# First routing phase with one operation between digits, and a changed order of side work in a fused retention, expert and gated-unit kernel

## The chip, the cores and the metric

The kernel runs on one core of a Trainium2 chip. The metric is the device time of one execution in microseconds (us), taken as the median of the runs shown. TensorE is PE in the profile (its weight loads PEld), VectorE is DVE, ScalarE is ACT, GpSimd is POOL, SyncE is SP. Each engine works through its own instructions in the order in which the program emits them; what one engine needs of another it waits for by semaphores.

## The reference, cut to what matters

Retention over 4 batches, 8 heads, 768 steps and 64 channels gives 3072 tokens of 512 values. The tokens are then dealt to 8 experts, and what the experts give goes through a gated unit with 1536 hidden columns:

```
logits = x @ w_gate                      # 3072 x 8
for idx in argsort(-logits.flatten()):   # best pair of token and expert first
    tok, e = idx // E, idx % E
    if assigned[tok] >= 0 or counts[e] >= cap: continue      # cap = 384
    assigned[tok] = e; counts[e] += 1
for e in range(E):
    out[assigned == e] = relu(x[assigned == e] @ w1[e]) @ w2[e]
gate = sigmoid(out @ w_gate2);  val = out @ w_val
return (gate * val) @ w_out
```

## The kernel before, in words

**Attention** (to about 154 us) works through 24 chunks of 128 tokens. In its spare time 23 of the 36 blocks of the gated unit's weights, which lie as 64-bit numbers in memory, are converted to 32 bits by `conv_steps`: step one is ACT L153 and DVE L154, step two DVE L156, step three ACT L158 and POOL L159, step four DVE L161. The other 13 are converted later (`late`, below).

**Routing** deals one expert at a time: the expert that fills up first, and its 384 tokens. `members(x)` does it. For the first expert (x = 0) nothing else can run beside it: five digits of a threshold are found one after the other (`widths`), each by three compares on DVE (`compare`, one for each third of the chunks in `parts`), 24 small matmuls (`count`, L284), a maximum (L587), a matmul with ones (L593) and two operations that make the next digit's column `edb` (L596, L598). `keep_busy` puts matmuls without use between them. Then a prefix sum (L624), another set of compares, a count and the row numbers `idx` (L651), with which three indirect DMAs on POOL's queue fetch the tokens (`gather`, L506).

For the later experts `members(x + 1)` runs while expert x computes, one step at each call of `hook()`; a step yields the number of hooks until the next. Its search has eight digits of 4 bits (`search4`): a compare (L291), three matmuls (L299), three DVE operations that end in `ex` (L301 to L304), a matmul (L318), then five more up to the next digit's compare (L321 to L291, L266). The member search that runs beside the first expert (x == 1) yields 2 hooks between `ex` and L318, the later ones 1.

**Expert and gated unit.** For each expert: 8 `h_step` and 8 `y_step` (w1 with ReLU, w2), then 12 rounds of `g_step` (two products, wg and wv) and `o_step` (wo). Every product is taken in three parts, so each weight block is split into a high part (ACT L664) and a remainder (DVE L665), up to 5 pieces ahead (`ahead`). Every step is some 12 matmuls, or 9 in `o_step`. A hook follows each step: 15 hooks in the `h_step` and `y_step` part (0 to 14), 15 and 16 in the first `g_step`, then three to a round: 17 + 3g, 18 + 3g and 19 + 3g. `h_step` and `y_step` emit what follows their matmuls (the ReLU and the remainder on DVE, the next pieces) and then the hook. `late` hangs the 13 remaining conversions on the hooks of the first expert, from hook 7 every 2.5 hooks. `turn_x` transposes the next expert's tokens (L673) from round 7 on, in the first expert from round 8.

The steps above for x == 1 place the fetch of its tokens at hook 40 and its first transpose right before hook 43; for later experts at hooks 33 and 40 (job[1] = 0; prep at hook 1; digit k's compare at hook 3 + 4k or 3 + 3k; the row numbers and the fetch 9 hooks after the last digit's compare).

**The end.** The last expert's three blocks of output are copied from PSUM (ACT, DVE, ACT) and scattered by three indirect DMAs on POOL's queue (L797).

Of the kernel before, what the change touches and what calls it, by code (L numbers as in the profile page):

```python
# [15 lines left out]
OP = mybir.AluOpType  # L16
# [4 lines left out]
def retention_moe_glu_kernel(  # L21
# [167 lines left out]
    bits = consts.tile([128, 2, NCH], I32, name="bits")  # L189
    far_up = consts.tile([128, NCH], F32, name="far_up")  # L190
    ones16 = consts.tile([128, 128], F16, name="ones16")
    same = consts.tile([128, 8], F32, name="same")
    spread = consts.tile([128, 16], F32, name="spread")

    def late_consts():
        im = dict(allow_small_or_imprecise_dtypes=True)
        POOL.iota(iota1, pattern=[[1, 128]], base=1, channel_multiplier=0, **im)
        POOL.iota(cp[:, :, 0], pattern=[[1, NCH]], base=0, channel_multiplier=0, **im)
        POOL.iota(cp[:, :, 1], pattern=[[0, NCH]], base=0, channel_multiplier=1, **im)
        POOL.iota(w8, pattern=[[-1, E]], base=E, channel_multiplier=0, **im)  # L200
        DVE.tensor_scalar(before, jp, 0.0, None, op0=OP.is_gt)
        DVE.tensor_scalar(after, jp, 0.0, None, op0=OP.is_lt)
        DVE.memset(ones, 1.0)
        DVE.memset(ones_r, 1.0)
        DVE.memset(ones16, 1.0)
        DVE.memset(bits[:, 0, :], -2147483648)
        DVE.memset(bits[:, 1, :], 15)
        DVE.memset(far_up, 512.0)
        DVE.tensor_reduce(same, ident.rearrange("p (t c) -> p c t", c=8), AX, OP.max)
        DVE.tensor_reduce(spread, ident.rearrange("p (t c) -> p t c", c=8), AX, OP.max)  # L210
        DVE.memset(free, 1.0)
        for t in cmp_tiles:
            POOL.memset(t, 0.0)
        DVE.tensor_copy(iox, iota1[:, :, None].to_broadcast([128, 128, NCH]))
        DVE.tensor_copy(arow, w8)
# [7 lines left out]
    NL = len(widths)  # L223
    parts = ((0, 8), (8, 16), (16, 24))
    first_part = ((0, 10), (10, 20), (20, 24))
# [81 lines left out]

    def search4(x):

        for n in range(8):  # L310
# [4 lines left out]
            ex = count4(cm)  # L315
            yield 2 if x == 1 else 1
            pd = psm.tile([128, 128], F32, name="pr")
# [119 lines left out]

    EARLY = 23
    LATE = [7 + 5 * n // 2 for n in range(NP - EARLY)]
    RAWS = 3  # L440
    conv_at = {4 + n * 41 // EARLY: n for n in range(EARLY)}
# [61 lines left out]

    idxs, xT, W, XG = {}, {}, {}, {}
    def gather(dst, src, col):
        POOL.indirect_dma_start(out=dst, out_offset=None, in_=src,  # L506
                                in_offset=bass.IndirectOffsetOnAxis(ap=col, axis=0))
# [32 lines left out]
    def fetch_rest():  # L540

        rest = W[0][0][:, :, 512:]
        ACT.activation(rest[:, 0, :1], ident[:, :1], AF.Copy)
        src = w1[bass.ds(which[0], 1)].rearrange("o (a p) f -> p (o a) f", p=128)
        SP.dma_start(rest, src[:, :, 512:])
        for f in range(2, W2R):
            fetch_w2(0, f)
        for n in range(RAWS):
            conv_load(EARLY + n, main, RAWS)

    which = {}

    def members(x, begun=None):
# [10 lines left out]
        if x < E - 1:  # L564
# [7 lines left out]
            for n in range(NL if x == 0 else 0):  # L572
# [6 lines left out]
                if n + 1 < NL:  # L579
                    digit(n + 1)  # L580
                yield 3 if T > 64 else 2
                pr = psm.tile([128, 128], F32, name="pr")
# [9 lines left out]
                if n + 1 < NL:  # L592
                    PE.matmul(pd[:, 0:1], ones[:T, :], fb[:T], start=True, stop=True)  # L593
                    wait(WA)
                    ed = small("ed")
                    DVE.tensor_scalar(ed, r["edb"], pd[:, 0:1], 512.0, op0=OP.subtract, op1=OP.mult)  # L596
                    r["edb"] = small("edb", dt=BF)
                    DVE.tensor_tensor(r["edb"], ed, r["dig"][:, n + 1, :], OP.add)  # L598
            if x == 0:
                full = pd[:, 0:E]  # L600
                PE.matmul(full, ones, fl, start=True, stop=True)
                wait(WC)
            else:
                yield from search4(x)
                full = r["full"]
# [14 lines left out]
        idxs[x] = idx  # L620
        DVE.tensor_scalar(which[x], mx[:1], -1.0, float(E), op0=OP.mult, op1=OP.add)
        sc = small("sc", (128, 2, NCH), BF)
        scf = sc.rearrange("p a c -> p (a c)")
        DVE.tensor_tensor_scan(scf, ones_r, AE.rearrange("p a c -> p (a c)"), 0.0, OP.mult, OP.add)  # L624
        fetch_weights(x)
        yield 2
# [16 lines left out]
        cms = [compare(i, c0, c1, 128, smb, OP.is_equal) for i, (c0, c1) in enumerate(parts)]  # L643
        yield 3 if x == 1 else 4
        ps = psm.tile([128, 128], F32, name="pr")
# [7 lines left out]
        if x + 1 < E:  # L653
            far = small("far")
            DVE.scalar_tensor_tensor(far, ai, NA - 0.5, free, op0=OP.is_gt, op1=OP.mult)
            DVE.scalar_tensor_tensor(free, ai, -0.5, free, op0=OP.is_lt, op1=OP.mult)
            DVE.tensor_tensor(free, free, far, OP.add)
            r["pen"] = small("pen", (128, E))
            DVE.tensor_scalar(r["pen"], w8, mx, -3.0e38, op0=OP.is_equal, op1=OP.mult)
            DVE.scalar_tensor_tensor(arow, arow, mx, arow, op0=OP.not_equal, op1=OP.mult)  # L660
        yield 1

# [35 lines left out]
    def make(n):  # L698
        while made[0] < min(n, len(order)):
# [11 lines left out]
            t = main.tile([128, 2, DT, 128], F32R, name="piece", bufs=RING)  # L711
            split(src, t[:, 0], t[:, 1], DVE)
            pieces[key] = t
# [18 lines left out]
    def h_step(x, f):  # L732
        w = use(("w1", x, f))
        p = psm.tile([128, CAP], F32, name="mm", bufs=3)
        for dt in range(DT):
            three(p, w, (xT[x][:, 0, dt, :], xT[x][:, 1, dt, :]), dt, dt == 0, dt == DT - 1)
        t = main.tile([128, 2, CAP], F32R, name="hT", bufs=2)
        ACT.activation(t[:, 0], p, AF.Relu)  # L738
# [4 lines left out]
    def y_step(x, f):  # L743
# [3 lines left out]
        for dt in range(DT):  # L747
            three(acc[0][dt], w, (hT[f][:, 0], hT[f][:, 1]), dt, f == 0, f == FB - 1)
        if f == FB - 1:
            t = main.tile([128, 2, DT, CAP], F32R, name="x2T")  # L750
            x2[0] = t
            for dt in range(DT):
                split(acc[0][dt], t[:, 0, dt, :], t[:, 1, dt, :])
        ahead(("w2", x, f))

    def g_step(x, g):
        t = x2[0]
        ps = []
        for kind in ("wg", "wv"):
            w = use((kind, x, g))  # L760
            p = psm.tile([128, CAP], F32, name="mm", bufs=3)
            for dt in range(DT):
                three(p, w, (t[:, 0, dt, :], t[:, 1, dt, :]), dt, dt == 0, dt == DT - 1)
            ps.append(p)
            hook()
            if kind == "wg":
                sg = main.tile([128, CAP], F32, name="sg", bufs=2)
                ACT.activation(sg, p, AF.Sigmoid)
        gv = main.tile([128, CAP], F32, name="gv", bufs=2)
        DVE.tensor_tensor(gv, ps[1], sg, OP.mult)  # L770
        gt = main.tile([128, 2, CAP], F32R, name="gT", bufs=2)
        split(gv, gt[:, 0], gt[:, 1])
        gT[g] = gt
        ahead(("wv", x, g))

    scat = []
    spacer = consts.tile([1, 1], F32, name="spacer")

    def o_step(x, g):
        w = use(("wo", x, g)).rearrange("p z a b -> p z (a b)")  # L780
        if g == 0:
            acc[1] = [psm.tile([128, M], F32, name="acc", bufs=4) for _ in range(NA)]
        for a in range(NA):
            r = slice(a * 128, (a + 1) * 128)
            p = acc[1][a]
            PE.matmul(p, gT[g][:, 0, r], w[:, 0], start=(g == 0), stop=False)  # L786
            PE.matmul(p, gT[g][:, 0, r], w[:, 1], start=False, stop=False)  # L787
            PE.matmul(p, gT[g][:, 1, r], w[:, 0], start=False, stop=(g == GB - 1))  # L788
        if g == GB - 1:
            for a in range(NA):  # L790
                o = main.tile([128, M], F32, name="o", bufs=3)
                if a % 2:
                    DVE.tensor_copy(o, acc[1][a])
                else:
                    ACT.activation(o, acc[1][a], AF.Copy)
                POOL.memset(spacer, 0.0)
                st = POOL.indirect_dma_start(  # L797
                    out=out, out_offset=bass.IndirectOffsetOnAxis(ap=idxs[x][:, a:a + 1], axis=0),
                    in_=o, in_offset=None)
                for s in scat:  # L800
                    tc.declare_no_dep(st.ins, s.ins, reason="rows of other tokens")
                scat.append(st)
        ahead(("wo", x, g))
# [28 lines left out]

    late = {}
    for n, u in enumerate(LATE):
        m = EARLY + n
        if n + RAWS < len(LATE):
# [5 lines left out]
    for x in range(E):  # L842
# [4 lines left out]
        for f in range(FB):  # L847
            if f + 1 < FB:
                h_step(x, f + 1)
                hook()  # L850
            y_step(x, f)
            hook()
        g_step(x, 0)
        turn = None
        for g in range(GB):
            if g + 1 < GB:
                g_step(x, g + 1)
            elif x + 1 < E:
                for _ in turn:
                    pass  # L860
                h_step(x + 1, 0)
            if g == (7 if x else 8) and x + 1 < E:
                assert job[0] is None
                turn = turn_x(x + 1)
            if turn is not None:
                next(turn, None)
            o_step(x, g)
            hook()

# [41 lines left out]
```

## Time and profile before

| | |
|---|---|
| median of 3 runs | 1124.16 us (1123.57 to 1124.96) |
| the profiled execution | 1123.29 us |
| its span from first to last instruction | 1121.5 us |
| mean granted TensorE clock | 0.99 of full speed |
| PE busy, share of the span | 1088.5 us, 97% |
| DVE busy | 736.8 us, 66% |
| ACT busy | 487.6 us, 43% |
| POOL busy | 134.9 us, 12% |

Busy shares are means over stages with different limits. PE's matmuls are pipelined and overlap in the records, so that 97% does not mean that PE is at its peak; matmuls without use count too.

### The profile page before, as it was taken

The numbers are of one execution on the slowest core, as the hardware profiler recorded it, in microseconds if no ns is written. First come the engines' busy times: TensorE is split into PE (matmuls) and PEld (weight loads), VectorE is DVE, ScalarE is ACT, GpSimd is POOL, SyncE is SP. The second block draws the span as 40 slices with busy tenths as digits, with TensorE's granted clock in tenths as the row PEclk, the third lists the DMA queues.
The fourth block names the chain that finished last, engine by engine and source line by source line (L and its number), as shares of the span: only waits on it lengthen the run. The fifth ranks groups of instructions, "written<-read, shape, count | busy, mean of one in ns | idle before, by whom it ended". The sixth has DMA issues, their size and how long they took to land.

```text
span 1121.5 us, 18122 instructions
## 1 busy us (share of the span) xinstructions
PE 1088.5 (97%) x6964; PEld 1005.2 (90%) x6964; DVE 736.8 (66%) x1787; ACT 487.6 (43%) x955; POOL 134.9 (12%) x146
## 2 busy tenths in 40 slices
PE   8999999988799999999999999999999999999997
PEld 6988988977799999989998999999989999999996
DVE  4887876888667756775677666765676545554542
ACT  3666623554343444334434343344343434343442
POOL 4354401121110011001100110011001000100001
PEclk9999989999899999999999999999999999999999
DMA  9999916123320212012100310031103012101000
GB/s 218 282 261 292 247 39 217 57 75 87 120 76 1 101 31 75 1 57 76 66 11 10 122 57 20 1 132 47 30 1 132 17 60 79 54 23 54 1 1 29
DMA packets 109608, 91.42 MB, mean 82 GB/s; under 512 B 54737, under 2 KB 92625, under 8 KB 109521
## 3 DMA queue, kind: packets, MB, share of 16 engines
q1 hardware_dynamic: 105680, 77.67, 23.4%
q0 software_dynamic: 3840, 12.59, 3.4%
q8 instruction: 55, 0.90, 0.3%
q14 instruction: 33, 0.26, 0.1%
HBM read 77.66 MB, written 12.58 MB: 80 GB/s over the span
## 4 chain that ended last, share of the span: by engine, by line
PE 73%; issue 11%; DVE 11%; SPq 2%; ACT 1%; DMA 1%; POOL 1%; POOLq 0%; DVEq 0%; ACTq 0%
PE mm L726 13%; PE mm L728 12%; PE mm L727 12%; PE acc L786 5%; PE acc L788 5%; PE acc L787 5%; DVE piece L665 3%; PE acc L726 2%; PE acc L728 2%; PE acc L727 2%; PE pA L373 2%; PE pY L388 2%; PE pX L407 2%; PE pS L395 2%; PE pY L384 2%
## 5 line engine op out<-in xcount | busy, mean ns | idle before, releaser
L726 PE MATMUL mm<-x2T,piece 128*128 128x384 f32 x768 | 261.7, 341 | 0.4 <-ACT x2T L664 0.4
L728 PE MATMUL mm<-x2T,piece 128*128 128x384 f32 x768 | 258.4, 337 | 0.7 <-DVE x2T L665 0.7
L727 PE MATMUL mm<-x2T,piece 128*128 128x384 f32 x768 | 257.6, 335 | 0.0
L665 DVE TENSOR_TENSOR piece<-wall,piece 128x512 fp32r<-128x512 f32 x288 | 186.2, 689 | 0.0
L664 ACT ACTIVATE gT<-gv 128x384 fp32r<-128x384 f32 x96 | 50.5, 526 | 266.5 <-DVE gv L770 266.5
L664 ACT ACTIVATE piece<-wall 128x512 fp32r<-128x512 f32 x288 | 163.1, 617 | 0.0
L726 PEld LDWEIGHTS mm<-x2T,piece 128*128 128x128 f32 x768 | 144.5, 188 | 3.8 <-ACT x2T L664 0.7
L727 PEld LDWEIGHTS mm<-x2T,piece 128*128 128x128 f32 x768 | 144.4, 188 | 3.1
L728 PEld LDWEIGHTS mm<-x2T,piece 128*128 128x128 f32 x768 | 144.1, 188 | 1.0 <-DVE x2T L665 1.0
L770 DVE TENSOR_TENSOR gv<-mm,sg 128x384 f32<-128x384 f32 x96 | 53.1, 553 | 129.1 <-PE mm L728 127.9
L786 PE MATMUL acc<-piece,gT 128*128 128x512 f32 x288 | 117.5, 408 | 0.0
L788 PE MATMUL acc<-piece,gT 128*128 128x512 f32 x288 | 114.0, 396 | 0.0
L787 PE MATMUL acc<-piece,gT 128*128 128x512 f32 x288 | 113.4, 394 | 0.0
L738 ACT ACTIVATE hT<-mm 128x384 fp32r<-128x384 f32 x64 | 31.5, 492 | 151.7 <-PE mm L728 151.7
L739 DVE SCALAR_TENSOR_TENSOR hT<-mm,hT 128x384 fp32r<-128x384 f32 x64 | 35.7, 557 | 87.1 <-ACT hT L738 87.0
L665 DVE TENSOR_TENSOR gT<-gv,gT 128x384 fp32r<-128x384 f32 x96 | 54.3, 566 | 56.9 <-ACT gT L664 56.9
L726 PE MATMUL mm<-xT,piece 128*128 128x384 f32 x256 | 87.5, 342 | 1.0 <-ACT xT L664 1.0
L726 PE MATMUL acc<-hT,piece 128*128 128x384 f32 x256 | 86.9, 339 | 0.0
L728 PE MATMUL mm<-xT,piece 128*128 128x384 f32 x256 | 86.2, 337 | 0.4 <-DVE xT L665 0.3
L727 PE MATMUL mm<-xT,piece 128*128 128x384 f32 x256 | 85.8, 335 | 0.0
L728 PE MATMUL acc<-hT,piece 128*128 128x384 f32 x256 | 85.8, 335 | 0.0
L727 PE MATMUL acc<-hT,piece 128*128 128x384 f32 x256 | 85.6, 334 | 0.0
(163 smaller groups left out, 1780.2 us busy)
## 6 DMA issues: line engine op xcount, KB each, us to landing
w2s<-in_moe_w_dram SPq DMA_DIRECT2D x64, 256.0 KB, 2.7
w1s<-in_moe_w_dram SPq DMA_DIRECT2D x7, 2048.0 KB, 7.7
q<-in_q_dram SPq DMA_DIRECT2D x12, 512.0 KB, 5.9
k<-in_k_dram SPq DMA_DIRECT2D x24, 256.0 KB, 5.6
v<-in_v_dram SPq DMA_DIRECT2D x24, 256.0 KB, 5.7
raw<-in_moe_w_gate_dram SPq DMA_DIRECT2D x12, 512.0 KB, 5.3
raw<-in_moe_w_val_dram SPq DMA_DIRECT2D x12, 512.0 KB, 5.4
xd<-xs SPq DMA_DIRECT2D x24, 256.0 KB, 4.4
```

The lines of the kernel that those rows point to most:

```text
L373: PE.matmul(ps[s][:, a, :], kT[i][r, a, :], q_of(i)[r, a, :], start=True, stop=True)
L664: ACT.activation(hi, src, AF.Copy)
L665: eng.tensor_tensor(lo, src, hi.bitcast(F32), OP.subtract)
L726: PE.matmul(p, w[:, 0, dt, :], r[0], start=start, stop=False)
L727: PE.matmul(p, w[:, 1, dt, :], r[0], start=False, stop=False)
L728: PE.matmul(p, w[:, 0, dt, :], r[1], start=False, stop=stop)
L738: ACT.activation(t[:, 0], p, AF.Relu)
L739: DVE.scalar_tensor_tensor(t[:, 1], p, 0.0, t[:, 0].bitcast(F32), op0=OP.max, op1=OP.subtract)
L770: DVE.tensor_tensor(gv, ps[1], sg, OP.mult)
L786: PE.matmul(p, gT[g][:, 0, r], w[:, 0], start=(g == 0), stop=False)
L787: PE.matmul(p, gT[g][:, 0, r], w[:, 1], start=False, stop=False)
L788: PE.matmul(p, gT[g][:, 1, r], w[:, 0], start=False, stop=(g == GB - 1))
```

## The change

It has seven parts.

1. First routing phase: the matmul with ones becomes one with 512 (`ones512`), `pre = 512 * edb + next digit` is made while PE counts, and one DVE operation instead of two makes the next `edb`. `parts` goes from 8, 8, 8 chunks to 6, 8, 10. The operation for `which` goes behind the prefix sum.
2. Three of the 13 late conversions move to the first routing phase: their loads are issued where the main pools are opened, and their steps by `fill` in stated places. Two last steps fall on hooks 0 and 1.
3. The other 10 are hung on hooks 7, 10, ... 34.
4. The search beside the first expert yields 1 hook between `ex` and L318, and 4 instead of 3 before the last count, as for the later experts; its `turn_x` starts at round 7.
5. In the first expert the 12 remainders of wo go to POOL.
6. Hooks go inside the steps: in `h_step`, `y_step` and `o_step` ahead of what follows the matmuls; in `g_step` the next pieces go ahead of the hook and of gv and gT.
7. The end: in the last expert the last gv and gT are made in three column blocks, the products of the last two rounds are interleaved (`last_blocks`), and each copy is halved between ACT and DVE.

```diff
-    parts = ((0, 8), (8, 16), (16, 24))
+    parts = ((0, 6), (6, 14), (14, 24))
...
-            yield 2 if x == 1 else 1
+            yield 1
...
-    EARLY = 23
-    LATE = [7 + 5 * n // 2 for n in range(NP - EARLY)]
-    RAWS = 3
+    EARLY, RAWS = 23, 3
+    LATE = [7 + 3 * n for n in range(NP - EARLY - RAWS)]
...
+    for n in range(RAWS):
+        conv_load(EARLY + n, main, RAWS)
+
+    fills = [[], [(0, 1)], [(0, 2)], [(1, 1)], [(0, 1)], [(1, 2), (2, 3)]]
+
+    def fill(x):
+        if x == 0:
+            for n, k in fills.pop(0):
+                conv_step(EARLY + n, k)
...
                 if n + 1 < NL:
                     digit(n + 1)
+                    pre = small("pre")
+                    DVE.scalar_tensor_tensor(pre, r["edb"], 512.0, r["dig"][:, n + 1, :], op0=OP.mult, op1=OP.add)
+                if n:
+                    fill(x)
                 yield 3 if T > 64 else 2
...
-                    PE.matmul(pd[:, 0:1], ones[:T, :], fb[:T], start=True, stop=True)
+                    PE.matmul(pd[:, 0:1], ones512[:T, :], fb[:T], start=True, stop=True)
                     wait(WA)
-                    ed = small("ed")
-                    DVE.tensor_scalar(ed, r["edb"], pd[:, 0:1], 512.0, op0=OP.subtract, op1=OP.mult)
                     r["edb"] = small("edb", dt=BF)
-                    DVE.tensor_tensor(r["edb"], ed, r["dig"][:, n + 1, :], OP.add)
+                    DVE.tensor_scalar(r["edb"], pre, pd[:, 0:1], None, op0=OP.subtract)
...
         cms = [compare(i, c0, c1, 128, smb, OP.is_equal) for i, (c0, c1) in enumerate(parts)]
-        yield 3 if x == 1 else 4
+        fill(x)
+        yield 4
...
+        fill(x)
         yield 1
...
-            split(src, t[:, 0], t[:, 1], DVE)
+            split(src, t[:, 0], t[:, 1], POOL if kind == "wo" and x == 0 else DVE)
...
@@ h_step
+        if f:
+            hook()
         t = main.tile([128, 2, CAP], F32R, name="hT", bufs=2)
...
@@ y_step
+        if f < FB - 1:
+            hook()
         if f == FB - 1:
...
+            hook()
         ahead(("w2", x, f))
...
@@ g_step
+            if kind == "wv":
+                ahead(("wv", x, g))
             hook()
...
+        last = x == E - 1 and g == GB - 1
+        for c in ([slice(a * 128, (a + 1) * 128) for a in range(NA)] if last else [slice(0, CAP)]):
+            DVE.tensor_tensor(gv[:, c], ps[1][:, c], sg[:, c], OP.mult)
+            split(gv[:, c], gt[:, 0, c], gt[:, 1, c])
         gT[g] = gt
-        ahead(("wv", x, g))
...
+    def store(x, a):
+        o = main.tile([128, M], F32, name="o", bufs=3)
+        if x == E - 1:
+            ACT.activation(o[:, :256], acc[1][a][:, :256], AF.Copy)
+            DVE.tensor_copy(o[:, 256:], acc[1][a][:, 256:])
...
+    def last_blocks(x):
+        for g, a in ((GB - 2, 0), (GB - 2, 1), (GB - 1, 0), (GB - 2, 2), (GB - 1, 1), (GB - 1, 2)):
+            o_products(x, g, a)
+            if g == GB - 1:
+                store(x, a)
...
-    late = {}
+    late = {0: [(conv_step, EARLY + 1)], 1: [(conv_step, EARLY + 2)],
+            3: [(conv_load, EARLY + RAWS + 1, main, RAWS), (conv_load, EARLY + RAWS + 2, main, RAWS)]}
...
-            if g == (7 if x else 8) and x + 1 < E:
+            if g == 7 and x + 1 < E:
                 turn = turn_x(x + 1)
```

## Rows read from the trace of the kernel before

**Rows 1.** View by stretches, of before: start:end, length, busy us (instructions) of each engine, clock, DMA

```profile
220.00:240.00 20.00, 18.22 (x102) 16.64 (x103) 18.20 (x45) 10.74 (x20) 4.26 (x3) 1.00 0.20 56
460.00:480.00 20.00, 19.55 (x116) 18.07 (x115) 14.71 (x47) 7.74 (x17) 0.00 (x0) 1.00 0.01 1
296.00:300.20 4.20, 4.20 (x13) 3.52 (x14) 1.29 (x2) 1.11 (x2) 0.41 (x2) 0.56 0.40 120
```

**Rows 2.** Timeline of ACT: start, length, engine, line, operation, [idle before, releaser]

```profile
218.82 1.61 ACT L664 ACTIVATE x2T<-acc 128x384 fp32r<-128x384 f32 x4
...
350.35 2.06 ACT L664 ACTIVATE x2T<-acc 128x384 fp32r<-128x384 f32 x4 [1.21 <-PE acc L728]
...
465.71 2.06 ACT L664 ACTIVATE x2T<-acc 128x384 fp32r<-128x384 f32 x4 [1.21 <-PE acc L728]
```

**Rows 3.** Waits of PE in 184:300: total us, times, longest

```profile
PE mm L673 <- DMA xg<-xd,idx: 6.1, 1, 6.1
PE pr L299 <- DVE cm L291: 4.0, 3, 1.5
PE pr L629 <- DVE sc L624: 1.4, 1, 1.4
PE pr L318 <- DVE ex L304: 1.1, 1, 1.1
```

**Rows 4.** Timeline of DVE in the first expert

```profile
229.23 0.22 DVE L301 TENSOR_TENSOR own<-pr,same 128x64 f32<-128x64 f32 x1
...
230.01 0.69 DVE L161 SCALAR_TENSOR_TENSOR wall<-raw,wall 128x512 f32<-128x512 f32 x1
...
235.37 0.28 DVE L321 TENSOR_REDUCE top<-pr 128x16 f32<-128x128 f32 x1
...
236.75 0.42 DVE L154 TENSOR_SCALAR wall<-raw 128x512 int32<-128x512 int32 x1
...
258.10 1.88 DVE L665 TENSOR_TENSOR piece<-wall,piece 128x512 fp32r<-128x512 f32 x3
```

**Rows 5.** Groups by line, 184:300: count, busy us, mean ns, idle before

```profile
L156 DVE SCALAR_TENSOR_TENSOR wall<-raw,wall 128x512 int32<-128x512 int32 x13 | 9.0, 692 | 0.4
L161 DVE SCALAR_TENSOR_TENSOR wall<-raw,wall 128x512 f32<-128x512 f32 x13 | 8.9, 683 | 0.0
...
L154 DVE TENSOR_SCALAR wall<-raw 128x512 int32<-128x512 int32 x13 | 5.5, 420 | 0.0
```

**Rows 6.** Tile view of ex in 200:292: ns min/median/max, first and last start

```profile
L304 DVE TENSOR_TENSOR ex<-spread,sm x8: 291/294/1116, 200.1 to 269.4; 128x128 f16<-128x128 f32 x8
```

**Rows 7.** Timeline of POOL

```profile
176.07 1.45 POOL L506 DMA_INDIRECT xg<-xd,idx  x1 [29.77 <-ACT piece L664]
...
223.78 1.31 POOL L159 TENSOR_TENSOR wall<-wall,raw 128x512 int32<-128x512 int32 x1 [3.81 <-DVE wall L156]
...
1113.22 0.96 POOL L797 DMA_INDIRECT out_dram<-o,idx  x1 [102.51 <-ACT o L795]
```

**Rows 8.** Waits of PE in 300:1000

```profile
PE pr L318 <- DVE ex L304: 3.8, 10, 0.5
```

**Rows 9.** Timeline of PE in the third expert

```profile
446.82 0.26 PE L299 MATMUL pr<-oh,cm 128*128 128x64 bf16 x3
...
449.12 0.23 PE L318 MATMUL pr<-ex,ones 128*128 128x128 f16 x1
...
453.42 0.26 PE L299 MATMUL pr<-oh,cm 128*128 128x64 bf16 x3
...
456.18 0.23 PE L318 MATMUL pr<-ex,ones 128*128 128x128 f16 x1 [0.31 <-DVE ex L304]
```

**Rows 10.** Timeline of PE and DVE in the first routing phase

```profile
156.12 0.24 DVE L596 TENSOR_SCALAR ed<-edb,pr 128x24 f32<-128x24 bf16 x1 [0.26 <-PE pr L593]
...
157.10 1.62 PE L284 MATMUL pr<-oh,cm 128*128 128x8 bf16 x24 [0.34 <-DVE cm L275]
...
162.12 1.46 PE L175 MATMUL acc<-busy 128*128 128x256 bf16 x6
```

More of the change, by code (lines that the diff above doesn't have):

```diff
@@ L190, in retention_moe_glu_kernel @@
     far_up = consts.tile([128, NCH], F32, name="far_up")
+    ones512 = consts.tile([128, 128], BF, name="ones512")
     ones16 = consts.tile([128, 128], F16, name="ones16")
@@ L205, in late_consts @@
         DVE.memset(ones16, 1.0)
+        DVE.memset(ones512, 512.0)
         DVE.memset(bits[:, 0, :], -2147483648)
@@ L306, in count4, with search4 @@
         return ex
-    def search4(x):
+    def search4():
         for n in range(8):
@@ L547, in fetch_rest @@
             fetch_w2(0, f)
-        for n in range(RAWS):
-            conv_load(EARLY + n, main, RAWS)
+        conv_load(EARLY + RAWS, main, RAWS)
     which = {}
@@ L603, in members @@
             else:
-                yield from search4(x)
+                yield from search4()
                 full = r["full"]
@@ L620, in members @@
         idxs[x] = idx
-        DVE.tensor_scalar(which[x], mx[:1], -1.0, float(E), op0=OP.mult, op1=OP.add)
         sc = small("sc", (128, 2, NCH), BF)
@@ L624, in members @@
         DVE.tensor_tensor_scan(scf, ones_r, AE.rearrange("p a c -> p (a c)"), 0.0, OP.mult, OP.add)
+        DVE.tensor_scalar(which[x], mx[:1], -1.0, float(E), op0=OP.mult, op1=OP.add)
         fetch_weights(x)
@@ L769, in g_step, with o_products @@
         gv = main.tile([128, CAP], F32, name="gv", bufs=2)
-        DVE.tensor_tensor(gv, ps[1], sg, OP.mult)
         gt = main.tile([128, 2, CAP], F32R, name="gT", bufs=2)
-        split(gv, gt[:, 0], gt[:, 1])
+        last = x == E - 1 and g == GB - 1
+        for c in ([slice(a * 128, (a + 1) * 128) for a in range(NA)] if last else [slice(0, CAP)]):
+            DVE.tensor_tensor(gv[:, c], ps[1][:, c], sg[:, c], OP.mult)
+            split(gv[:, c], gt[:, 0, c], gt[:, 1, c])
         gT[g] = gt
-        ahead(("wv", x, g))
     scat = []
     spacer = consts.tile([1, 1], F32, name="spacer")
+    def o_products(x, g, a):
+        w = use(("wo", x, g)).rearrange("p z a b -> p z (a b)")
+        r = slice(a * 128, (a + 1) * 128)
+        p = acc[1][a]
+        PE.matmul(p, gT[g][:, 0, r], w[:, 0], start=(g == 0), stop=False)
+        PE.matmul(p, gT[g][:, 0, r], w[:, 1], start=False, stop=False)
+        PE.matmul(p, gT[g][:, 1, r], w[:, 0], start=False, stop=(g == GB - 1))
+    def store(x, a):
[3 more added lines that the diff above has]
+            DVE.tensor_copy(o[:, 256:], acc[1][a][:, 256:])
+        elif a % 2:
+            DVE.tensor_copy(o, acc[1][a])
+        else:
+            ACT.activation(o, acc[1][a], AF.Copy)
+        POOL.memset(spacer, 0.0)
+        st = POOL.indirect_dma_start(
+            out=out, out_offset=bass.IndirectOffsetOnAxis(ap=idxs[x][:, a:a + 1], axis=0),
+            in_=o, in_offset=None)
+        for s in scat:
+            tc.declare_no_dep(st.ins, s.ins, reason="rows of other tokens")
+        scat.append(st)
+    def last_blocks(x):
[3 more added lines that the diff above has]
+                store(x, a)
     def o_step(x, g):
-        w = use(("wo", x, g)).rearrange("p z a b -> p z (a b)")
         if g == 0:
@@ L783, in o_step @@
         for a in range(NA):
[L784 to L788, printed above, removed]
+            o_products(x, g, a)
+        hook()
         if g == GB - 1:
             for a in range(NA):
[L791 to L802, printed above, removed]
+                store(x, a)
         ahead(("wo", x, g))
@@ L831, in retention_moe_glu_kernel @@
     h_step(0, 0)
-    late = {}
+    late = {0: [(conv_step, EARLY + 1)], 1: [(conv_step, EARLY + 2)],
+            3: [(conv_load, EARLY + RAWS + 1, main, RAWS), (conv_load, EARLY + RAWS + 2, main, RAWS)]}
     for n, u in enumerate(LATE):
-        m = EARLY + n
+        m = EARLY + RAWS + n
         if n + RAWS < len(LATE):
@@ L849, in retention_moe_glu_kernel @@
                 h_step(x, f + 1)
-                hook()
             y_step(x, f)
-            hook()
         g_step(x, 0)
@@ L866, in retention_moe_glu_kernel @@
                 next(turn, None)
+            if x == E - 1 and g >= GB - 2:
+                if g == GB - 1:
+                    last_blocks(x)
+                continue
             o_step(x, g)
-            hook()
 _INS = ["q", "k", "v", "moe_w_gate", "moe_w1", "moe_w2", "moe2_w_gate", "moe2_w_val", "moe2_w_out"]
```

## The prediction

> **What bounds the kernel now.** I read the stretches first, then the waits, then single rows. Between 350.35 and 465.71 one expert with a search beside it takes 115.36 us, measured from one x2T to the next; the first expert, from 218.82 to 350.35, takes 131.53 [rows 2]. So 16.2 us are lost in the first expert. The stretches show by what: at 220:240 DVE is busy 18.20 of 20 us and PE gets through 102 instructions, in a later expert 14.71 and 116 [rows 1]. PE's waits name two things [rows 3]. It stands 6.1 us for the fetched tokens of the second expert, and 4.0 + 1.4 + 1.1 = 6.5 us for what the search makes on DVE. After the first of these the granted clock is 0.56 over 4.20 us [rows 1], the two levels of 1.2 and 2.4 GHz mixed; the idle 6.1 us went before it. Outside the first expert PE waits little: ten times for ex, 3.8 us [rows 8]. The first routing phase is a chain of DVE and PE with nothing beside it, and the end hangs on three stores.
>
> **Part by part.**
>
> The fetch of the second expert's tokens (part 4). It moves from hook 40 to 33, the first transpose from ahead of hook 43 to ahead of hook 40. The distance grows from 3 hooks to 7. A hook is about 2.15 us (two of them 4.30, 449.12 to 453.42 [rows 9]), so 8.6 us are added to a margin that was short by 6.1. The later experts have the same 33 and 40, and no such wait stands among theirs [rows 8]. Gone are 6.1 us and what the low clock cost, (1 - 0.56) x 4.20 = 1.85 us: **-8.0**. POOL's queue now has wo remainders ahead of the fetch; one of them, some 1.3 us (as 223.78 [rows 7]), would be hidden by the 2.5 us that are left over, and would cost 1.3 without that.
>
> DVE beside the search (parts 3, 4, 5). Durations of a round of three hooks: a digit of the search is 230.01 - 229.23 = 0.78 and 236.75 - 235.37 = 1.38, so 2.16 [rows 4]; a conversion is 0.42 + 0.69 + 0.68 = 1.79 on DVE [rows 5]; a piece is 1.88 / 3 = 0.63 [rows 4]. A POOL operation also holds DVE up: ex, 0.29 long, once took 1.12 [rows 6], so one POOL operation costs DVE between 0 and 0.82. I take the middle, 0.41, since the median of ex is undisturbed and its worst is not rare among so few. Before, a round held three quarters of a digit and 1.2 conversions; after, one digit and one conversion, and a piece less. Change per round: 0.25 x 2.16 = +0.54, -0.2 x (1.79 + 0.41) = -0.44, -0.63 + 0.41 = -0.22; together -0.1. So DVE remains as full as it was as long as the search lasts, and PE loses as much per round. But the search lasts less long: from hook 15 its prefix sum is awaited at hook 29 instead of 37, that is 4.7 rounds instead of 7.3. 6.5 x 4.7 / 7.3 = 4.2 us stay: **-2.3**. Bounds: all 6.5 go, or, since ex has one hook instead of two, 3 us more are lost. Behind each waiting L318 or L299 stand PE's products, and for these DVE's gv and gT wait.
>
> One page of the Trainium skill speaks against part 5. The row is that of ex: 0.29 us alone, 1.12 at worst, while POOL's operation runs 1.31 [rows 6, 7]. "SBUF — State Buffer", section "SBUF: two separate sides", says that VectorE with two SBUF inputs and GpSimd share a port pair as an exclusive lock that the first holds for its whole instruction. The trace agrees that one side blocks, up to 0.82 here. By the rule with each hold counted in full, two POOL operations in each of 4.7 rounds cost DVE 1.31 instead of 0.41, 4.7 x 2 x 0.90 = 8.5 us more, and the sum would be 1117.0; by the middle of the rows it is 1108.5. Rival E below is that case by the rows alone.
>
> Three conversions less in the first expert (part 2). Their relief is in the count of conversions per round above; in the first routing phase they stand where DVE waits for PE's count, and after the row numbers, where POOL issues three DMAs of 0.96 to 1.45 [rows 7], over 3 us for some 1.7 of DVE's work (0.69 + 0.42 + 0.69 [rows 5]). Without that cover three times 1.79 would be on the path. Two costs I put in: POOL's add of 1.31 meets the fifth digit's compares (0 to 0.82, taken 0.25, as DVE reaches them late in it), and the first fetch, which took 1.45 beside DVE work and 0.96 for a like one at the end [rows 7], may slow down the second one too (0 to 0.5, taken 0.35). The loads are queued on SP ahead of the first weights, which SP can't ask for before `which` is known anyway.
>
> First routing phase (part 1). PE stood 0.34 before the second digit's count [rows 10], DVE's removed operation is 0.24 [rows 10], and the first compare is a quarter smaller: -0.34 there, and -0.2 at the next digit. At the third gap PE's six useless matmuls last 1.46, to 163.58 [rows 10], and the count starts right behind them, so that a faster DVE gives 0. In the fifth digit DVE sets the pace, and two more matmuls come behind the last third, 2 x 1.62 / 24 = 0.14: what the removed operation gives is used up by them and the add above. The prefix sum ahead of `which` gives 0.1. Together -0.6 with 0.6 of costs: **0**, between -1.1 and +1.2.
>
> Hooks inside the steps (part 6). In later experts L318 comes 2.30 after L299 when ex is in time (446.82, 449.12), 2.76 when not, of which the idle time is 0.31 [rows 9]; a wait costs 0.46 / 0.31 = 1.5 times its idle time. Ten waits with 3.8 idle [rows 8] cost 3.8 to 5.6. They come where own, sm and ex stand behind a remainder that waits for ACT and behind a piece of 0.63, or behind x2T and a piece. With the hook first these are behind. I take **-5.0**, bounds 0 and -5.6. What is queued behind the hook now is hT, and its reader waits for 24 more matmuls, 4.30 us; a hook has at most 1.38 on DVE, in the first expert 1.1 more. So the cover holds; if it did not, every `h_step` would wait.
>
> The end (part 7). Each store takes 0.96 on POOL [rows 7], and the last follows the first by two of them. The first now needs DVE's half of the copy, which stands behind gv and gT of all three blocks: **0**, within half a store, 0.5, either way.
>
> Sum against the profiled execution of 1123.29: -8.0 - 2.3 - 5.0 + 0 + 0 = -15.3, 1108.0. It lies 0.9 under the median of the runs, 1124.16, which the same sum brings to 1108.9. I say **1108.5** for the median.
>
> **Rivals.**
>
> A, the pace is too fast: ex now has one hook, and in each of the eight digits PE waits as long as it once did at most, 1.5 [rows 3]: 12 us in place of 6.5, with the fetch and the later experts as above: 1123.3 - 8.0 + 5.5 - 5.0 = 1115.8. For it: DVE is no less full. Against it: the later experts keep this pace, but at 14.71 of 20.
>
> B, the ten waits stay: DVE is as late with ex, since pieces now stand ahead of the hook in `g_step`. Then 1108.5 + 5 = 1113.5. For it: DVE has no less to do. Against it: the piece that is passed is longer than the 0.46 lost.
>
> C, slower than before: hT comes too late behind the hook's work in each of eight `h_step`s of the six experts with a search. At 0.5 us each, 48 x 0.5 = 24 us, it would be 1132; from 0.32 each (15.3 / 48) it decides. Against it: hT's 4.30 us of room.
>
> D, the change doesn't do what it says: the fetch is as late as ever, because DVE falls as far behind as the seven hooks gained, and what the other parts give is lost with it: 1122 to 1125. Against it: PE waits for DVE at every L299 and L318, so DVE can't fall 15 us behind.
>
> E, the holds are long: each POOL operation stops DVE for 0.82, the worst of [rows 6], and there are two to a round now: 4.7 x 2 x (0.82 - 0.41) = 3.9 us more, 1112.4. For it: DVE has more operations with two inputs than any other kind. Against it: the median of ex is undisturbed, though 13 POOL operations ran.
>
> **Chances and range.** The forecast (1103.5 to 1111) has 0.60, A 0.14, B 0.12, E 0.08, C 0.04, D 0.02. All terms at their good bounds: 8.0 + 6.5 + 5.6 + 1.1 + 0.5 = 21.7, 1102; A stands at 1115.8, B and E at 1113.5 and 1112.4. The range is 1103.5 to 1115. Less than 0.2%, 2.2 us, is about what the measurement can't tell from no change. Faster 0.94, same 0.02 (D), slower 0.04 (C).
>
> **What would show it.** L673 of the second expert without a wait; the granted clock at full from there on; waits of PE for ex, cm and sc in the first expert of about 4 us; ten waits for ex in the later ones gone, and 114.3 instead of 115.36 from x2T to x2T; the first transposes no more than 1 us earlier or later. The prediction fails if the first expert still takes over 125 us from x2T to x2T, or if a later one takes more than before.

## The result and the profile after

The changed kernel takes 1111.27 us (1111.02 to 1112.49) where the kernel before takes 1124.32 beside it: ratio 0.9886, 95% interval 0.9869 to 0.9903. That is 2.8 us over the forecast of 1108.5: inside the range of 1103.5 to 1115, and 0.3 over the stretch of 1103.5 to 1111 that the forecast itself had. The profiled execution has a span of 1109.3 us. It divides by the starts of the first count, of the first product on `xT` and of the first and second x2T:

| stretch | before | after | difference | predicted |
|---|---|---|---|---|
| attention, to the first count | 153.55 | 155.05 | +1.50 | (same code) |
| first routing phase, to the first product | 30.52 | 30.36 | -0.16 | 0 |
| first half of the first expert, to its x2T | 34.75 | 33.98 | -0.77 | with the next: |
| x2T to x2T beside the first search | 131.53 | 124.04 | -7.49 | -8.0 - 2.3 |
| the rest, to the end | 771.15 | 765.87 | -5.28 | -5.0 + 0 |
| span | 1121.5 | 1109.3 | -12.2 | -15.3 |

Attention has the same instructions in both; its end moves between executions (last section). Without it the sum is -13.7.

The stretches of after (columns as in [rows 1]: the five pairs are PE, PEld, DVE, ACT, POOL):

```profile
200.00:220.00 20.00, 19.86 (x121) 18.71 (x120) 17.92 (x50) 9.99 (x20) 2.96 (x2) 1.00 0.28 95
220.00:240.00 20.00, 16.96 (x98) 14.85 (x96) 17.50 (x45) 11.81 (x22) 7.23 (x6) 1.00 0.26 78
240.00:260.00 20.00, 16.86 (x91) 14.76 (x92) 17.35 (x44) 7.64 (x15) 7.00 (x5) 1.00 0.18 53
260.00:280.00 20.00, 18.33 (x114) 16.32 (x112) 16.22 (x39) 8.64 (x17) 7.69 (x6) 1.00 0.49 178
280.00:300.00 20.00, 20.00 (x111) 18.55 (x111) 13.93 (x20) 10.94 (x22) 8.01 (x6) 1.00 0.11 34
```

The clock of 0.56 is gone: 1.00 from 200 to 300. What stays is at 220:260, where PE gets through 98 and 91 instructions; POOL's share (fifth pair) is the new thing. The waits of PE in 175:300 of after, answering [rows 3]:

```profile
PE pr L320 <- DVE ex L306: 5.2, 4, 1.6
PE acc L807 <- ACT gT L679: 1.7, 2, 1.3
PE mm L743 <- DVE x2T L680: 0.8, 1, 0.8
PE mm L688 <- issue: 0.7, 1, 0.7
```

The fetched tokens (now L688) are waited for no more. But the search takes 5.2 + 1.7 = 6.9 us (the second stands behind gT, which DVE makes late), not the predicted 4.2. In 300:1000 the same view has no row at all: the ten waits of [rows 8] are gone. The x2T of after on ACT ([rows 2]) come 114.25 us apart in later experts, as predicted (114.3):

```profile
219.39 2.06 ACT L679 ACTIVATE x2T<-acc 128x384 fp32r<-128x384 f32 x4 [0.90 <-PE acc L743]
...
343.43 2.06 ACT L679 ACTIVATE x2T<-acc 128x384 fp32r<-128x384 f32 x4 [1.23 <-PE acc L743]
...
457.68 2.06 ACT L679 ACTIVATE x2T<-acc 128x384 fp32r<-128x384 f32 x4 [1.23 <-PE acc L743]
```

Why the search still stops PE is seen in one round. The timeline of DVE, then that of POOL, then that of PE, in after:

```profile
238.05 0.68 DVE L680 TENSOR_TENSOR piece<-wall,piece 128x512 fp32r<-128x512 f32 x1
238.65 0.22 DVE L303 TENSOR_TENSOR own<-pr,same 128x64 f32<-128x64 f32 x1
238.90 0.27 DVE L305 TENSOR_REDUCE sm<-own 128x8 f32<-128x64 f32 x1
239.20 0.83 DVE L306 TENSOR_TENSOR ex<-spread,sm 128x128 f16<-128x128 f32 x1
240.28 1.45 DVE L680 TENSOR_TENSOR piece<-wall,piece 128x512 fp32r<-128x512 f32 x1 [0.25 <-ACT piece L679]
241.65 0.28 DVE L323 TENSOR_REDUCE top<-pr 128x16 f32<-128x128 f32 x1
```
```profile
238.26 1.62 POOL L159 TENSOR_TENSOR wall<-wall,raw 128x512 int32<-128x512 int32 x1 [5.37 <-issue]
239.84 1.33 POOL L680 TENSOR_TENSOR piece<-wall,piece 128x512 fp32r<-128x512 f32 x1
```
```profile
231.72 0.23 PE L320 MATMUL pr<-ex,ones 128*128 128x128 f16 x1 [0.56 <-DVE ex L306]
240.09 0.23 PE L320 MATMUL pr<-ex,ones 128*128 128x128 f16 x1 [1.62 <-DVE ex L306]
248.41 0.23 PE L320 MATMUL pr<-ex,ones 128*128 128x128 f16 x1 [1.57 <-DVE ex L306]
256.66 0.23 PE L320 MATMUL pr<-ex,ones 128*128 128x128 f16 x1 [1.48 <-DVE ex L306]
```

POOL's add runs to 239.88 and holds ex, its wo remainder runs to 241.17 and holds the next piece: 0.83 instead of 0.29, 1.45 instead of 0.68, together 1.31 us of a round of 8.3 (a round is the distance of two L320). own and sm, which ran beside the add too, were not held (0.22 and 0.27; 0.22 in [rows 4]). Rows of the first routing phase, DVE and then POOL ([rows 10] of before):

```profile
157.62 0.24 DVE L611 TENSOR_SCALAR edb<-pre,pr 128x24 bf16<-128x24 f32 x1 [0.26 <-PE pr L608]
...
166.42 0.93 DVE L611 TENSOR_SCALAR edb<-pre,pr 128x24 bf16<-128x24 f32 x1 [0.25 <-PE pr L608]
```
```profile
166.03 1.30 POOL L159 TENSOR_TENSOR wall<-wall,raw 128x512 int32<-128x512 int32 x1 [18.08 <-PE pr L286]
```

The one operation that is left between digits takes 0.24, and 0.93 where the moved conversion's add is under way: 0.69 that the faster digits have to pay back ("Part 1 undone", below). The -0.16 of the table can't be read to that accuracy: in the nine profiles here whose instructions in this stretch are those of after, it takes 29.90 to 33.13 us.

### The profile page after: what moved, and what is told of

Read it like the earlier page. It is cut to its first block, busy times and chain, and to the rows that moved or that the text cites. A ratio compares the mean times of both kernels' runs of the same rounds, so it can differ in the third digit from the quotient of the medians.

```text
span 1109.3 us, 18222 instructions
## 1 busy us (share of the span) xinstructions
PE 1085.4 (98%) x6964; PEld 1004.0 (91%) x6964; DVE 742.4 (67%) x1782; ACT 490.2 (44%) x958; POOL 150.6 (14%) x158
## 4 chain that ended last, share of the span: by engine, by line
PE 77%; issue 10%; DVE 7%; SPq 2%; ACT 1%; DMA 1%; POOL 1%; POOLq 0%; ACTq 0%; DVEq 0%
PE mm L741 13%; PE mm L743 13%; PE mm L742 13%; PE acc L807 5%; PE acc L809 5%; PE acc L808 5%; PE acc L741 3%; PE acc L743 3%; PE acc L742 3%; PE pA L375 2%; PE pY L390 2%; DVE piece L680 2%; PE pS L397 2%; PE pY L386 2%; PE pX L409 2%
## 5 line engine op out<-in xcount | busy, mean ns | idle before, releaser
L680 DVE TENSOR_TENSOR piece<-wall,piece 128x512 fp32r<-128x512 f32 x276 | 190.1, 713 | 106.3 <-ACT piece L679 103.7
L679 ACT ACTIVATE piece<-wall 128x512 fp32r<-128x512 f32 x288 | 169.2, 621 | 0.0
L679 ACT ACTIVATE gT<-gv 128x384 fp32r<-128x384 f32 (+1 forms) x98 | 50.8, 519 | 212.2 <-DVE gv L796 212.2
L790 ACT ACTIVATE sg<-mm 128x384 f32<-128x384 f32 x96 | 47.1, 491 | 136.1 <-PE mm L743 113.3
L680 DVE TENSOR_TENSOR gT<-gv,gT 128x384 fp32r<-128x384 f32 (+1 forms) x98 | 54.2, 553 | 62.3 <-ACT gT L679 62.3
L517 POOL DMA_INDIRECT xg<-xd,idx x24 | 24.7, 1029 | 445.1 <-issue 434.0
```

The lines of the kernel that those rows point to most:

```text
L517: POOL.indirect_dma_start(out=dst, out_offset=None, in_=src, in_offset=bass.IndirectOffsetOnAxis(ap=col, axis=0))
L679: ACT.activation(hi, src, AF.Copy)
L680: eng.tensor_tensor(lo, src, hi.bitcast(F32), OP.subtract)
```

## The experiments

Times are medians, ratios are to the kernel before on the same chip. "First expert" is the stretch from x2T to x2T (131.53 before, 124.04 after), "first half" the stretch ahead of it (34.75, 33.98), "later" that from there to the end (771.15, 765.87). Stretches come from one profiled execution each. The kernel before took 1123.48 to 1124.96 us beside the runs below, so two medians from different chips can differ by some 1.5 us for that reason alone. The edits are cut to the lines that matter.

**Part 6 undone.** Hooks and pieces as before, all else changed (`y_step` and `o_step` likewise).

```diff
 def h_step:   three(...)
-        if f: hook()
         t = main.tile(... "hT")
...
 def g_step:
-            if kind == "wv": ahead(("wv", x, g))
             hook()
...
         gT[g] = gt
+        ahead(("wv", x, g))
```

> The changed kernel with part 6 undone: hooks and pieces stand where they stood before. My theory: the reorder is worth 5 us in the later experts (ten waits for ex, one x2T-to-x2T stretch 115.4 instead of 114.25) and next to nothing in the first expert, so the ten waits come back, the first expert stays at 124 us from x2T to x2T, and the time is 1111.3 + 5 = 1116. Rival, order: the reorder is what makes ex late in the first expert, where pieces stand ahead of the hook; then the first expert gets shorter by 2 us or more and the time is 1114 or less.

1124.65 (1122.69 to 1128.34), ratio 1.0006 (0.9994 to 1.0017): no gain is left. Later 770.59, first expert 129.92, first half 35.92: 12.5 us more than after in the three, 7.8 of them in the first half and the first expert. Both expectations fail. PE waits 9.2 us for ex, 2.7 for POOL's piece and 2.1 for POOL's add ahead of the first transposes, in 175:300:

```profile
PE pr L320 <- DVE ex L306: 9.2, 7, 2.4
PE acc L802 <- POOL piece L680: 2.7, 2, 2.1
PE mm L688 <- POOL wall L159: 2.1, 1, 2.1
```

**Part 5 undone.** All remainders on DVE.

```diff
-            split(src, t[:, 0], t[:, 1], POOL if kind == "wo" and x == 0 else DVE)
+            split(src, t[:, 0], t[:, 1], DVE)
```

> The changed kernel with part 5 undone: the first expert's 12 wo remainders are on DVE again. Theory, a round held by POOL: in a round of 8.3 us the two POOL operations hold DVE for some 1.3 us, about half of it the remainder's; without it DVE loses 0.7 less to holds and has 0.63 more to do, so the first expert stays within 1 us of 124 and the time within 1 us of 1111.3. Rival, the port is held in full: each remainder costs DVE 1.31, and without the twelve the time falls by 3 us or more, to 1108. Rival, relief: POOL takes real work off DVE, and the time rises by 2 us or more.

1108.39 (1106.69 to 1109.62), 0.986 (0.9843 to 0.9876). Part 5 costs 2.9 us, and 3.2 in the first expert (120.88). The theory fails; the time is that of the first rival, but not by its reason, as the rows above show holds of 0.54 and 0.77 and not of 1.31. PE's waits for ex are 3.9 us instead of 5.2, rounds 7.8 (L320 at 233.47, 241.27, 249.11), and DVE makes two pieces in 1.28 where it made one in 1.45.

**Part 4 undone.**

```diff
-            yield 1
+            yield 2 if x == 1 else 1
...
-        yield 4
+        yield 3 if x == 1 else 4
...
-            if g == 7 and x + 1 < E:
+            if g == (7 if x else 8) and x + 1 < E:
```

> The changed kernel with part 4 undone: two hooks between ex and L320 beside the first expert, row numbers at hook 40, first transpose ahead of hook 43. Theory: PE's waits for the search fall from 5.2 us to 3 or less, but the wait for the fetched tokens comes back, 2 to 5 us as DVE has less to do than before, with 1 to 2 us of low clock behind it: time 1112 to 1116. Rival, pace: the one hook is the only thing that costs, the fetch comes in time with the lighter DVE, and the time is 1108 or less. Rival, fetch only: the wait for the tokens comes back whole, 6 us and 1.85 of low clock, and the time is 1117 or more.

1115.23, 0.9927 (0.991 to 0.9944). The time fits, the wait does not: tokens cost PE 0.2. It waits for the tail of a search that lasts longer (`which` 2.7, cm 2.5, ex 2.4), and the clock is 0.91 in two stretches of 20 us.

**Parts 2 and 3 undone.** 13 conversions in the first expert, every 2.5 hooks; the loads and steps in the first routing phase go too. The two parts were not undone singly.

```diff
-    LATE = [7 + 3 * n for n in range(NP - EARLY - RAWS)]
+    LATE = [7 + 5 * n // 2 for n in range(NP - EARLY)]
```

> The changed kernel with parts 2 and 3 undone: none of the 13 late conversions in the first routing phase, one each 2.5 hooks from hook 7 on. Theory: a round beside the search has 1.2 conversions instead of one, some 0.5 us more on DVE in 4 to 5 rounds, so the first expert grows by 2 to 4 us; the first routing phase gets shorter by the hold on the fifth digit's edb, 0.7; time 1112.5 to 1115. Rival, pace: conversions don't matter to the wait for ex, and the time stays within 1 us of 1111.3 or falls by the 0.7.

1119.09, 0.996 (0.9946 to 0.9974): 7.8 us, more than either expectation. First expert 130.22, first half 35.77, ex 6.7 us of waits, and a clock of 0.91 and 0.93 in two stretches of 20 us.

**Part 6 alone**, on the kernel before.

> The kernel before with part 6 alone. Theory, two places: the later experts gain their 5.1 us (the ten waits for ex), and in the first expert the fetch stays late, 6 us with 1.85 of low clock, as it stands at hooks 40 and 43: 1124 - 5 = 1119, 1117.5 to 1120.5. Rival, the order is all: the changed kernel lost 8 us in its first half and first expert when the order was put back, so the order alone gives most of that as well, 1124 - 13 = 1111 to 1113. Rival, order only with the rest: no gain in the first expert and a loss in it, as pieces now stand ahead of the hook, 1121 or more.

1122.73, 0.9983 (0.997 to 0.9995). Later 766.24 (-4.9), but the first expert 134.27 (+2.7), with a wait of 7.4 for the tokens. The third expectation holds.

**Part 4 alone**, on the kernel before.

> The kernel before with part 4 alone: one hook between ex and L318, row numbers at hook 33, first transpose ahead of hook 40. Prediction: the fetch wait and its low clock go, 8 us, at no more than 5.5 us of longer search waits: 1116 to 1121.5. Rival, what the order put back showed: with hooks behind the pieces each of the eight digits waits 1.3 to 2.4 us for ex and the clock falls on the way, so that what the fetch gave is lost, 1122 to 1126.

1120.35, 0.9954 (0.9936 to 0.9971). The token wait goes, first expert 125.51; ex now stops PE 7.5 us (7 times, at most 3.2) and the first half is 37.43. Later 771.31. The time is within the prediction; the rival's longer waits for ex are there, but they don't eat up what the fetch gave.

**The adds one hook earlier**, part 5 undone.

```diff
-    LATE = [7 + 3 * n for n in range(NP - EARLY - RAWS)]
+    LATE = [6 + 3 * n for n in range(NP - EARLY - RAWS)]
```

> The changed kernel with wo's remainders on DVE (as in e2) and the late conversions one hook earlier, at hooks 6, 9, ... 33, so that POOL's add runs beside gv and the idle 0.6 us behind it and not beside ex. Theory, hold by place: ex takes 0.29 instead of 0.83, a round of 7.8 us becomes 7.3, and four to five rounds give 2 to 2.5 us: 1106. Rival, hold anywhere: another operation with two inputs (gT or a piece) is held instead, the round stays 7.8 and the time 1108.4 within 0.8.

1112.91 (1111.34 to 1115.87). ex is unheld, 0.291 to 0.294 us in all eight, but gT is held instead (0.72 to 0.81 for 0.56), and the rounds stay at 7.8 to 7.9: the hold moves, it does not go. So the rival has the mechanism, but not the time, which is worse than 1108.39 by 4.5 us (2.8 by the ratios). In the stretches it is 3.8 us (first half 35.62 for 33.83, first expert 122.91 for 120.88), with waits for hT (1.4) and for POOL's add ahead of the transposes (1.4), and a clock of 0.92 in 260:280.

**Part 1 undone.**

```diff
-    parts = ((0, 6), (6, 14), (14, 24))
+    parts = ((0, 8), (8, 16), (16, 24))
...
-                    DVE.tensor_scalar(r["edb"], pre, pd[:, 0:1], None, op0=OP.subtract)
+                    DVE.tensor_scalar(ed, r["edb"], pd[:, 0:1], 512.0, op0=OP.subtract, op1=OP.mult)
+                    DVE.tensor_tensor(r["edb"], ed, r["dig"][:, n + 1, :], OP.add)
```

> The changed kernel with part 1 undone: two operations between digits, equal thirds, the operation for the first weights ahead of the prefix sum; the conversions stay where they are. Prediction's term of part 1 without the conversions' costs: 0.6 slower, 1111.9, and the hold of 0.69 on the fifth digit's operation stays. Rival, full worth: PE is not what sets the digits' pace and all four operations of 0.28 count, 1.2 slower or more, 1112.5. Rival, thirds: two more matmuls behind the last third cost as much as the operation gives, 1111.3 within 0.3.

1110.24 (1110.15 to 1110.66), 0.9867 (0.9849 to 0.9884): 1.0 us less than after, with overlapping intervals of the ratio. None of the three expectations has this time; what gives the change its name is worth nothing in the medians. The start of the row numbers shows more. They stand near the end of the phase, ahead of the fetch: before, after, then with parts 2 and 3 undone, then with part 1 undone:

```profile
174.94 0.16 DVE L651 SCALAR_TENSOR_TENSOR idx<-sl 128x3 int32<-128x3 f32 x1
```
```profile
176.59 0.16 DVE L665 SCALAR_TENSOR_TENSOR idx<-sl 128x3 int32<-128x3 f32 x1
```
```profile
174.86 0.16 DVE L663 SCALAR_TENSOR_TENSOR idx<-sl 128x3 int32<-128x3 f32 x1
```
```profile
175.77 0.16 DVE L665 SCALAR_TENSOR_TENSOR idx<-sl 128x3 int32<-128x3 f32 x1
```

The first count starts at 153.55, 155.05, 154.21 and 153.76, so the row numbers come 21.39, 21.54, 20.65 and 22.01 us behind it (21.31 to 21.35 in the other eight runs with the digits and conversions of after). Part 1 alone takes 0.74 off, the three conversions put 0.7 to 0.9 back. Most of what varies between executions lies behind the row numbers, from the fetch to the first product.

**The gap filled**, part 5 undone: the hook that carries a digit goes between gv and the remainder of gT, where DVE waits 0.65 us for ACT in every round.

```diff
-            hook()
             if kind == "wg":
+                hook()
...
-            split(gv[:, c], gt[:, 0, c], gt[:, 1, c])
+            ACT.activation(gt[:, 0, c], gv[:, c], AF.Copy)
+            if c.start == 0:
+                hook()
+            DVE.tensor_tensor(gt[:, 1, c], gv[:, c], gt[:, 0, c].bitcast(F32), OP.subtract)
```

> The changed kernel with the wo remainders back on VectorE (1108.4 us) and the third hook of a round moved between gv and its remainder gT, where VectorE idles 0.65 us per round waiting for ScalarE. Theory (VectorE sets the round of the search in the first expert: its work fills 7.2 of the 7.8 us of a round, and the rest is this gap): rounds of about 7.2 us, L320 waits of 0.3 to 0.5 instead of 0.8 to 1.1, four rounds x 0.65: 1105.5 to 1106.5. Rival (TensorE's wait is for the order of the work before ex, not for VectorE's sum): rounds stay at 7.8, 1107.5 to 1109.

1105.69 (1103.65 to 1108.11), 0.9841 (0.9819 to 0.9863), the fastest here. First expert 117.70. PE's L320 shows rounds of 7.1 and waits of 0.4:

```profile
230.54 0.23 PE L320 MATMUL pr<-ex,ones 128*128 128x128 f16 x1 [0.38 <-DVE ex L306]
237.67 0.23 PE L320 MATMUL pr<-ex,ones 128*128 128x128 f16 x1 [0.36 <-DVE ex L306]
244.80 0.23 PE L320 MATMUL pr<-ex,ones 128*128 128x128 f16 x1 [0.38 <-DVE ex L306]
```

The stretches 220:240 and 240:260 show what fills such a round: DVE is busy 19.35 and 19.37 of 20 us (17.50 and 17.35 in after).

```profile
220.00:240.00 20.00, 18.32 (x101) 15.95 (x101) 19.35 (x52) 11.83 (x22) 4.78 (x3) 1.00 0.24 79
240.00:260.00 20.00, 19.36 (x108) 17.17 (x107) 19.37 (x52) 10.46 (x20) 4.92 (x3) 1.00 0.31 95
```

DVE's sum sets the round: the theory holds, by the rounds. The medians alone (2.7 us, 2.1 by the ratios) have overlapping intervals.

**Parts 5 and 6 undone** together.

> The changed kernel without parts 5 and 6 (wo remainders on VectorE, hooks as before): it keeps the first phase, the conversions and the pace. If the parts add up: 1124.65 less the 2.9 that part 5 costs with the new order, 1121 to 1122.5. Rival (under the old order the GpSimd remainder is what TensorE waits for, 2.7 us for the piece and most of the 9.2 us at L320, so part 5 without part 6 costs much more than 2.9): 1115 to 1119, with the later experts still 770.5.

1117.08, 0.9944 (0.9928 to 0.9961). Under the old order part 5 costs 7.6 us (1124.65 - 1117.08; 6.7 in the first expert, 123.22 for 129.92), under the new one 2.9: the rival has the price. Its reason holds in half. The waits for POOL's piece and add (2.7 and 2.1) are gone, and so are stretches with a clock of 0.91 and 0.92 between 240 and 300; but most of the wait for ex was not POOL's remainder, for it stays:

```profile
PE pr L320 <- DVE ex L306: 8.6, 7, 1.8
```

Later 770.6.

**The late adds left out**, part 5 undone.

```diff
-        POOL.tensor_tensor(wi, wi, lo, OP.add)
+        if m < 26:
+            POOL.tensor_tensor(wi, wi, lo, OP.add)
```

> The changed kernel with the wo remainders on VectorE, and with GpSimd's addition left out of the conversions of the first expert's stage (their low words are not added, so the weights of these blocks are not rounded as in the reference). It prices the hold of VectorE by GpSimd alone. Theory (ex takes 0.83 us beside the addition and 0.29 alone, and VectorE sets the round): ex 0.29, rounds of 7.3, four rounds x 0.54: 1105.5 to 1107. Rival (the hold only uses up time in which VectorE would have waited): rounds 7.8, within 1 us of 1108.4.

1105.94 (1105.5 to 1109.57), 0.9849 (0.9828 to 0.987). ex takes 0.29, the first expert 119.05, 1.8 less than with the add. The rounds are 7.5 to 7.7 rather than 7.3: with ex early, DVE waits 0.27 for ACT's high part of the next piece. So of a hold of 0.54 a round gives back 0.1 to 0.3, and 0.27 is time that DVE then waits for ACT. The median is in the theory's range, the rounds lie between the two; the median's gain of 2.45 (1.2 by the ratios) has overlapping intervals.

**Half of part 6 undone**: the old order in the wg, wv and wo steps, the new one in the w1 and w2 steps.

> The changed kernel with only the second half of part 6 undone: in the wg/wv/wo steps the hooks and the order of the pieces as before, in the w1/w2 steps the new place. It asks where the 13 us of part 6 lie. Theory (the search of the first expert that TensorE waits for runs beside the wg/wv/wo steps, L320 at 231 to 257 us, x2T of the first expert at 219): the 5.9 us of the first expert come back and the first half keeps its 34, part of the later experts' 4.7 comes back: 1116 to 1121, waits for GpSimd's piece at the wo products again. Rival (the hook ahead of hT in the w1/w2 steps does it): 1111 to 1113.5 with the first expert at 124 to 126.

1114.96, 0.9916 (0.9899 to 0.9933), between the theory and the rival. Later 765.88: the w1 and w2 half carries all of the later experts' gain. First expert 127.60, 3.6 more than after. DVE's timeline shows why:

```profile
244.27 0.56 DVE L680 TENSOR_TENSOR gT<-gv,gT 128x384 fp32r<-128x384 f32 x1 [0.59 <-ACT gT L679]
245.31 1.96 DVE L680 TENSOR_TENSOR piece<-wall,piece 128x512 fp32r<-128x512 f32 x2 [0.48 <-ACT piece L679]
247.19 0.68 DVE L161 SCALAR_TENSOR_TENSOR wall<-raw,wall 128x512 f32<-128x512 f32 x1
247.79 0.41 DVE L154 TENSOR_SCALAR wall<-raw 128x512 int32<-128x512 int32 x1
248.24 0.69 DVE L156 SCALAR_TENSOR_TENSOR wall<-raw,wall 128x512 int32<-128x512 int32 x1
248.85 0.22 DVE L303 TENSOR_TENSOR own<-pr,same 128x64 f32<-128x64 f32 x1
249.10 0.28 DVE L305 TENSOR_REDUCE sm<-own 128x8 f32<-128x64 f32 x1
249.42 1.10 DVE L306 TENSOR_TENSOR ex<-spread,sm 128x128 f16<-128x128 f32 x1
```

Two pieces stand ahead of ex, where the new order has one. The first of them is held by POOL's remainder (1.96 for the two instead of 1.28), and the add holds ex for longer (1.10 where it took 0.83). PE also waits 2.1 for POOL's piece, as the theory has it. Rounds are 9.1 us (L320 at 232.34, 241.45, 250.57).

## Why the prediction was right, and where it was off

**The fetch and the low clock, -8.0.** Both are gone: no wait for tokens, clock 1.00. Part 4 alone removes the wait, as the step says ("Part 4 alone"). It is not the only way: with the other parts in place the wait is as good as gone without it (0.2), and PE stands at the tail of the search instead. The first expert's two stretches give -8.26.

**DVE beside the search, -2.3.** This step failed in size: 6.9 us of waits stay, not 4.2, so the term was about 0. Its number at fault is the 0.41 for one POOL operation, the middle between two ends. The rounds show 0.54 for the add and 0.77 for the remainder, with 0.25 of waiting for ACT between them. That makes part 5 a loss of 2.9 us where the sum counted it as a gain of 0.22 a round. With part 5 undone 3.9 us of waits for ex stay, near the 4.2 of the sum. The rows of before said more than the median of [rows 6]: three of the eight ex were held (0.84, 0.83 and 1.12 long, at 219.28, 238.98 and 269.36), not one. Rival E had the mechanism and, at 1112.4, nearly the time.

The "SBUF: two separate sides" section of the Trainium skill's page "SBUF — State Buffer" says that one side has the shared port pair for its whole instruction and the other waits. This trace agrees: the held instructions end behind POOL's (ex at 240.03, the add at 239.88), and the add itself, which starts while a piece of DVE is under way, takes 1.62 where 1.31 is usual [rows 7]. The prices were off on both sides: 0.41 in the sum is too little, and 1.31 each, the hold counted in full, is too much. DVE pays only what is left of POOL's operation when its next instruction of that kind starts, and a little less: ex lost 0.54 of the 0.68 that were left, the piece 0.77 of 0.90, ex in the run with part 6 undone 0.97 of 1.11. The difference is 0.13 to 0.14 each time.

**The later experts, -5.0.** Right: -5.28 with the end. Part 6 does it (e5, -4.9), and the w1 and w2 half of it is enough (e12).

**The first routing phase and the end, 0.** Right: -0.16, and from the last x2T to the end 84.28 instead of 84.47. The sum's -0.6 for the digits and 0.6 for the conversions are there in the row numbers too (-0.74, and 0.7 to 0.9). Part 7 was not undone in any run; its worth is read from the end's stretch alone.

**The rivals.** A: with the new order the faster pace does not cost, undoing it costs 4.0. B: no wait for ex is left after 300 us. C: no wait for hT in after. D: the tokens are in time.

**What the sum missed** is that the parts don't add. Undone one at a time they are worth 13.4 (part 6), 7.8 (2 and 3), 4.0 (4), -2.9 (5) and nothing (1), 22.3 in all, of a gain of 13.05. Without part 6 the others together gain nothing (1124.65), though part 4 alone gains 4.6 and all but parts 5 and 6 gain 6.4: under the old order it is part 5 that takes the gain away. The sum counted part 6 in the later experts alone. Beside the first expert, where the sum has nothing for it, undoing it costs 7.8 us, while on the kernel before it lengthens that expert by 2.7. So that the sum came within 2.8 us is in part luck: the first expert, at 124.04, is 1 us from the 125 at which the prediction said that it fails. And the low clock comes on top: 0.91 over a stretch of 20 us is 1.8 us more.

## What to carry to other kernels

Moving work to GpSimd is no relief for VectorE by itself: price it by what is left of GpSimd's operation when VectorE's next instruction of a held kind starts. To let it end beside instructions that are not held would cost nothing by these rows, but no run here brought that about; an add one hook earlier only held another instruction. Where one engine's sum sets the round, first look what stands ahead of the instruction that the other engine waits for, and for the gap in which it waits itself: order was worth 13.4 us here and filling a gap of 0.65 us in each round some 2 to 3 (1108.39 to 1105.69; 3.2 in the first expert), the moved operations less than nothing. Parts that relieve the same wait are priced together, each with the others in place.

## What the runs showed of the hardware that was not expected

The granted clock falls behind waits much shorter than the 6.1 us of [rows 3]. Rows of the stretch 240:260 with the parts 5 and 6 undone (longest wait of PE 1.8), then with half of part 6 undone (2.4):

```profile
240.00:260.00 20.00, 14.76 (x82) 12.66 (x81) 17.23 (x41) 8.46 (x16) 3.86 (x3) 1.00 0.26 79
```
```profile
240.00:260.00 20.00, 15.48 (x76) 13.42 (x77) 16.30 (x36) 8.32 (x16) 6.42 (x5) 0.90 0.24 79
```

The first is at 2.4 GHz throughout; the second has part of its time at 1.2 GHz, and (1 - 0.90) x 20 = 2.0 us are lost by it. The longest wait does not decide it alone. In the run with the adds one hook earlier no wait of PE in 175:300 is over 1.6, and the clock falls all the same:

```profile
260.00:280.00 20.00, 18.33 (x104) 15.93 (x103) 17.39 (x49) 8.92 (x18) 2.60 (x2) 0.92 0.45 172
```

What decides it these runs don't settle.

Attention, the same instructions in every kernel here, ended between 153.08 and 158.66 us in the fourteen profiles. So a single execution is compared by its stretches, and a difference under some us of span by medians.
